# Sigmoid attention and a two-layer block with silu: h of batches 2 to 7 by pairs of batches in seven block products, with the next pair's attention in the out layer's time

## The chip, the core and the metric

The kernel runs on one core of one Trainium2 chip. The metric is the device time in microseconds; the kernel before takes 381.18 us (median of three runs, 381.03 to 382.37). Engines: TensorE (PE; PEld is its loading of weights), VectorE (DVE), ScalarE (ACT), GpSimd (POOL) and SyncE (SP). In this kernel GpSimd only issues loads, and SyncE issues stores and DMA transposes.

## What is computed

```python
# q, k, v: (8, 12, 448, 64) float32; w_in (768, 2048), w_out (2048, 768)
scores = q @ k.T / 8 - log(448)
attn   = sigmoid(scores)                  # no softmax
x      = (attn @ v), heads side by side   # (8 * 448, 768)
h      = x @ w_in
out    = (h * sigmoid(h)) @ w_out         # (3584, 768) float32
```

## The kernel before

**Attention.** The 12 heads of a batch are six pairs; a "quad" g is two pairs (three quads per batch, NQB = 24), and each quad has seven chunks of keys (NCH = 7), so a batch has 21 units (g, ch), NT_B. `scores` (L169) makes one unit: four matmuls of 64 x 64 x 448 into a tile of `ps_sc` (two PSUM buffers), and one Sigmoid on ScalarE (L183) into `attnT` (12 buffers). `values` (L193) takes the seven units of a quad, 28 matmuls into two tiles `pav` of `ps_1`, and VectorE copies them to `xT` (L218), scaled by 64. `ps_1` has four PSUM buffers for everything else. q and k of a quad must be transposed: for quads 0 to 5 by TensorE (L147); from 6 on by `dma_transpose` (L158): one copy into rows (`kr`, `qr`, three buffers) by ScalarE or VectorE, then a DMA transpose issued by SyncE into `kT`, `qT` (four buffers).

**h.** `h_unit` (L229) makes 128 columns of h for one batch: six matmuls (448 columns) into `ps_1`, a Sigmoid on ScalarE (L247), and the product on VectorE (L248) into `gTr`, which holds two batches.

**out.** `out_set` (L288) makes two 128-row blocks of out with seven block products of eight matmuls (384 columns) in place of eight, by sums of blocks: of g (`S1` to `S4`, VectorE, L318 to L327), of w_out (`T`, once, L277), and of the products (`plus`, L314, VectorE; one copy M1 by ScalarE, L321). Two batches have seven blocks, three sets; a seventh block is put into `kept` (L374) and forms a set with the next pair's.

**The order** is written out by hand, and each engine takes its instructions in that order. `all_moe` (L379) is a generator of h units and out sets; each `yield` gives the nanoseconds of one matmul (189 or 163). The main loop (L541) issues two units of scores, the values of a quad that is complete, a row copy if one is due, and then lets the generator run for `paces` nanoseconds (`stretch`, L398). So the attention of batch b + 1 is spread over the h and out of earlier batches. Before batch 2's scores (n = 42) stands one long stretch of 21500 ns, in which h of batches 0 and 1 ends; there ScalarE also copies the rows of quads 6, 7 and 8 (`by_h1`, L355), and VectorE makes the sums of w_out.

**Loads** go through GpSimd's queue in program order: after quad 2's values come v of quad 5, two quarters of w_out, then k and q of quads 6 and 7 (L449 to L454).

Of the kernel before, what the change touches and what calls it, by code (L numbers as in the profile page):

```python
# [2 lines left out]

# [14 lines left out]
def kernel(  # L18
# [9 lines left out]
    nc = tc.nc  # L28
# [93 lines left out]

    def new_qkT(g):
        for name in ("k", "q"):
            qkT[name, g] = p4.tile([P, NCH, P], F16, tag=f"{name}T", name=f"{name}T")

    dummy = cpool.tile([P, 512], F16, tag="dummy", name="dummy")

# [29 lines left out]
    def dma_transpose(g, name, copy):  # L158
        if ("k", g) not in qkT:
            new_qkT(g)  # L160
        rows = p3.tile([P, NCH, 2, D], F16, tag=f"{name}r", name=f"{name}r")
        copy(rows, flat[name, g].rearrange("p j c d -> p c j d"))  # L162
        nc.sync.dma_start_transpose(
            out=qkT[name, g], in_=rows.rearrange("p c j d -> p (c j d)")
        )
# [27 lines left out]
    def values(g, end=NCH):  # L193
        b, iq = divmod(g, NQ)
        if b not in xT:
            assert b < 2 or b - 2 in h_done
            xT[b] = p2.tile([P, NPAIR, S], F16, tag="xT", name="xT")
        pav, done_rounds = part_of.pop(g, None) or (
            [ps_1.tile([P, 512], F32, tag="ps1", name="pav") for _ in range(2)],
            0,  # L200
        )
        for ch in range(done_rounds, end):
            at = attnT.pop((g, ch))
            for half in range(2):
                own = slice(half * HP, (half + 1) * HP)
                for j in range(2):
                    nc.tensor.matmul(  # L207
                        pav[half][j * D : (j + 1) * D, :S],
                        flat["v", g][own, j, ch, :],
                        at[own, j, :],  # L210
                        start=(ch == 0),
                        stop=(ch == NCH - 1),
                    )
        if end < NCH:
            part_of[g] = pav, end
            return
        for half in range(2):
            nc.vector.tensor_scalar_mul(xT[b][:, half * NQ + iq, :], pav[half][:, :S], SX)  # L218
        if iq == NQ - 1:
            ready.add(b)  # L220

# [7 lines left out]
    def h_unit(b, fc):  # L229
        nonlocal hold  # L230
        hold = b > 0 and fc == NFC - 1
        ph = ps_1.tile([P, 512], F32, tag="ps1", name="ph")
        for at, cc in enumerate(pairs):
            assert b in ready or at < 4
            nc.tensor.matmul(  # L235
                ph[:, :S],
                w_in_sb[:, cc, fc * P : (fc + 1) * P],
                xT[b][:, cc, :],
                start=(at == 0),
                stop=(at == NCC - 1),  # L240
            )
            if at < NCC - 1:
                yield 189
        if fc == NFC - 1:
            h_done.add(b)
        tsig = p3.tile([P, S], F16, tag="tsig", name="tsig")
        nc.scalar.activation(tsig, ph[:, :S], AF.Sigmoid, bias=0.0, scale=ISX)  # L247
        nc.vector.tensor_mul(  # L248
            gTr[:, fc, (b % 2) * S : (b % 2) * S + S], ph[:, :S], tsig
        )  # L250
        yield 189

    rows_of = out.rearrange("(b p c) e -> b c p e", b=B, c=NCH)

# [27 lines left out]
    def block(g):  # L282
        return gTr[:, :, g * P : (g + 1) * P]
# [1 line left out]
    def row_blocks(m, g):  # L285
        return [rows_of[2 * m + u // NCH, u % NCH] for u in (2 * g, 2 * g + 1)]

    def out_set(a1, rows1, a2, rows2, last=False):  # L288
        nonlocal hold
        lo, hi = slice(0, NHC), slice(NHC, NFC)  # L290
        osb = [p4.tile([P, DMODEL], F32, tag="osb", name="osb") for _ in range(2)]
        c11, c12 = (osb[0][:, nh * NO2 : (nh + 1) * NO2] for nh in range(2))
        c21, c22 = (osb[1][:, nh * NO2 : (nh + 1) * NO2] for nh in range(2))
        m1 = p2.tile([P, NO2], F32, tag="m1", name="m1")
        sg = [cpool.tile([P, NHC, P], F16, tag=f"S{i}", name=f"S{i}") for i in range(1, 5)]

        def store(rows, o, cols, engines):
            for at, (row, eng) in enumerate(zip(rows, engines)):
# [1 line left out]

        left, right, whole = slice(0, NO2), slice(NO2, DMODEL), slice(0, DMODEL)

        def product(a, w):
            po = ps_1.tile([P, 512], F32, tag="ps1", name="po")
            for fc in range(NHC):
                nc.tensor.matmul(  # L306
                    po[:, :NO2], a[:, fc, :], w[:, fc, :], start=(fc == 0), stop=(fc == NHC - 1)
                )
                if fc < NHC - 1:
                    yield 163  # L310
            return po[:, :NO2]

        def plus(o, po, x, sign=ISX):
            nc.vector.scalar_tensor_tensor(  # L314
                out=o, in0=po, scalar=sign, in1=x, op0=ALU.mult, op1=ALU.add
            )

        nc.vector.tensor_sub(sg[2], a1[:, lo], a2[:, lo])  # L318
        nc.vector.tensor_add(sg[0], a2[:, lo], a2[:, hi])
        po = yield from product(a1[:, lo], wq[0][0])  # L320
        nc.scalar.activation(m1, po, AF.Copy, scale=ISX)  # L321
        nc.vector.tensor_sub(sg[1], sg[0], a1[:, lo])
        hold = False
        yield 163
        po = yield from product(a1[:, hi], wq[1][0])
        plus(c11, po, m1)
        nc.vector.tensor_sub(sg[3], a1[:, hi], sg[1])  # L327
        if last:
            store(rows1, osb[0], left, (nc.sync, nc.sync))
        yield 163  # L330
        po = yield from product(sg[2], tw[3])
        plus(c22, po, m1)
        yield 163
        po = yield from product(sg[1], tw[2])
        plus(c22, po, c22)
        plus(c12, po, m1)
        yield 163
        po = yield from product(a2[:, hi], tw[4])
        plus(c21, po, c22, -ISX)
        yield 163  # L340
        po = yield from product(sg[0], tw[1])
        plus(c22, po, c22)
# [9 lines left out]
        yield 163  # L352


    by_h1 = {3: 6, 6: 7, 9: 8}  # L355
    early = [h_unit(0, fc) for fc in range(2)]
    sums = w_sums()

    def moe_h(b):
        for fc in range(NFC):  # L360
            yield from early[fc] if b == 0 and fc < 2 else h_unit(b, fc)
            if b == 1:
                if fc >= 2:
                    next(sums)
                if fc in by_h1:
                    for name in ("k", "q"):
                        dma_transpose(by_h1[fc], name, act_copy)

    def moe_set(m, g):
        step = out_set(block(g), row_blocks(m, g), block(g + 1), row_blocks(m, g + 1))  # L370
        for i, ns in enumerate(step):
            if m % 2 == 0 and g == 2 and i % 8 == 4 and i < 32:
                fcs = slice(i // 8 * 4, i // 8 * 4 + 4)
                nc.scalar.activation(kept[:, fcs], block(NCH - 1)[:, fcs], AF.Copy)  # L374
            if m == 0 and g == 0 and i in (10, 14):
                next(sums)
            yield ns

    def all_moe():  # L379
        for m in range(B // 2):  # L380
            yield from moe_h(2 * m)
            if m > 0:
                yield from moe_set(m, 0)
            yield from moe_h(2 * m + 1)
            if m == 0:
                yield from moe_set(m, 0)
            yield from moe_set(m, 2)
            yield from moe_set(m, 4)
            if m % 2 == 1:
                g = NCH - 1  # L390
                yield from out_set(
                    kept, row_blocks(m - 1, g), block(g), row_blocks(m, g), m == B // 2 - 1
                )

    stream = all_moe()
# [44 lines left out]
    def after_values(g):  # L440
# [18 lines left out]
                load("kq", to)  # L459
        if g == 5:  # L460
            load("kq", 9)
        if g >= 6 and g + 3 < NQB:
            later.extend(((g + 3, "k"), (g + 3, "q")))

    later = []

    def rows_if_any():
        if later:
            g, name = later.pop(0)
            dma_transpose(g, name, nc.vector.tensor_copy)  # L470
            if name == "q" and g + 4 < NQB and g + 4 > 12:
                load("kq", g + 4)

    def values_if_any():
        if waiting:
            g = waiting.pop(0)
            values(g)
            after_values(g)

    keep_busy(9)  # L480
    pe_transpose(
# [23 lines left out]
    def begin(fc, steps):  # L505
        for _ in range(steps):
            next(early[fc])
# [28 lines left out]
        for do, *what in behind.get(n, ()):  # L536
            do(*what)

    paces = {1: 1600, 2: 2000, 3: 2550, 4: 3400, 5: 3400, 6: 3000, 7: 3000}
    stretch(paces[1])  # L540
    for n in range(NT_B + 3, len(units), 2):  # L541
        burst = units[n : n + 2]
        if n == 2 * NT_B:
            values_if_any()
            stretch(21500)
        for u in burst:
            scores(*u)
        values_if_any()
        rows_if_any()
        for g, ch in burst:  # L550
            if ch == NCH - 1:
                waiting.append(g)
        if n in (24, 30):
            transposes(4 + (n - 24) // 6, "k")
        elif n in (26, 32):
            transposes(4 + (n - 26) // 6, "q")
        stretch(paces[1] if 1 not in ready else paces[n // NT_B])
    for g in waiting:
        values(g)
    for _ in stream:  # L560
        pass

# [29 lines left out]
```

## Time and profile before

| | us |
|---|---|
| median of 3 runs | 381.18 |
| the profiled execution's time | 381.95 |
| its span | 380.2 |
| TensorE busy | 370.8 |
| VectorE busy | 235.2 |
| ScalarE busy | 225.9 |
| L235 (h), 768 matmuls, busy | 153.2 |
| L183 (Sigmoid of scores), 168 | 144.2 |
| L248 (product with the sigmoid), 128 | 78.9 |
| L247 (Sigmoid of h), 128 | 68.6 |
| L314 (sums of out's products), 112 | 60.7 |

The profile is one execution. Its span runs from the first to the last instruction, and the time has 1.75 us around it. Busy times count each instruction from start to end; matmuls overlap, so that 353 ns of a matmul of h are more than the distance from one to the next. The page cuts the span into 40 slices and gives the busy share of each in tenths. The chain of waits goes back from the last instruction, at each step to what released it. In a timeline, columns are start, duration, engine, line, operation, tiles and count; the brackets give the idle time before it and what ended it.

### The profile page before, as it was taken

What the parts mean: (1) busy time and instruction counts of PE and PEld (TensorE: products, weight loads), DVE (VectorE), ACT (ScalarE), POOL (GpSimd) and SP (SyncE); (2) the same over time, 40 slices, a digit from 0 to 9 for tenths busy, and PEclk for the clock granted to TensorE, in tenths of its full rate; (3) what the DMA queues carried; (4) which work ended last, traced back from release to release, by engine and by line L of the source; (5) the groups of instructions that cost most, each with busy time, mean ns of one, the idle gap of its engine ahead of it and who ended that gap; (6) DMA issues with size and microseconds to landing.
All of it is one profiled execution on the core that took longest, in us unless ns stands there. A gap on an engine that the chain in (4) does not pass through costs nothing.

```text
span 380.2 us, 7666 instructions
## 1 busy us (share of the span) xinstructions
PE 370.8 (98%) x3083; PEld 186.0 (49%) x3083; DVE 235.2 (62%) x416; ACT 225.9 (59%) x329; POOL 93.5 (25%) x158
## 2 busy tenths in 40 slices
PE   7989999999999999999999999999999999999995
PEld 2444445545554445445555444544455444555563
DVE  2636646987565666566766647735757446656773
ACT  4988875757667764777434576477764776054000
POOL 8946325403752323122221303101100000000000
PEclk9999999999999999999999999999999999999999
DMA  7999999995999947945939949536347300110233
GB/s 125 177 185 204 205 204 171 133 140 110 165 241 216 151 56 99 173 54 69 162 67 183 132 78 121 71 86 74 48 85 97 84 3 2 50 34 0 82 85 83
DMA packets 66403, 42.80 MB, mean 113 GB/s; under 512 B 37056, under 2 KB 62912, under 8 KB 66368
## 3 DMA queue, kind: packets, MB, share of 16 engines
q0 software_dynamic: 28032, 22.59, 43.2%
q1 hardware_dynamic: 38112, 19.41, 28.5%
q8 instruction: 24, 0.39, 0.4%
q10 hardware_dynamic: 224, 0.33, 0.3%
q14 instruction: 11, 0.09, 0.1%
HBM read 45.61 MB, written 11.01 MB: 149 GB/s over the span
## 4 chain that ended last, share of the span: by engine, by line
PE 78%; DMA 13%; POOL 3%; DVE 3%; ACT 2%; issue 1%; ACTq 0%; POOLq 0%
PE po L306 34%; PE ph L235 29%; PE psc L176 8%; PE pav L207 6%; DMA w_in_sb<-in_moe_w_in_dram 5%; DMA w_out_sb<-in_moe_w_out_dram 5%; DMA qf<-in_q_dram 1%; DMA vf<-in_v_dram 1%; POOL kf L78 1%; DVE gTr L248 1%; DVE T L277 1%; POOL qf L78 1%; ACT qr L137 1%; POOL vf L78 1%; ACT attnT L183 0%
## 5 line engine op out<-in xcount | busy, mean ns | idle before, releaser
L183 ACT ACTIVATE attnT<-psc 128x896 f16<-128x896 f32 x168 | 144.2, 918 | 59.9 <-PE psc L176 59.8
L235 PE MATMUL ph<-xT,w_in_sb 128*128 128x448 f16 x768 | 153.2, 353 | 1.2 <-DMA w_in_sb<-in_moe_w_in_dram 1.2
L248 DVE TENSOR_TENSOR gTr<-ph,tsig 128x448 f16<-128x448 f32 x128 | 78.9, 623 | 70.1 <-ACT tsig L247 68.6
L235 PEld LDWEIGHTS <-w_in_sb 128*128 128x128 f16 x768 | 71.9, 98 | 77.1 <-issue 12.8
L247 ACT ACTIVATE tsig<-ph 128x448 f16<-128x448 f32 x128 | 68.6, 547 | 54.4 <-PE ph L235 53.7
L78 POOL DMA_DIRECT2D vf<-in_v_dram x48 | 28.9, 624 | 136.4 <-PE pav L207 136.4
L306 PEld LDWEIGHTS <-S 128*128 128x128 f16 x448 | 42.3, 98 | 33.9 <-issue 6.8
L314 DVE SCALAR_TENSOR_TENSOR osb<-po,osb 128x384 f32<-128x384 f32 x70 | 37.6, 554 | 25.2 <-PE po L306 24.5
L176 PE MATMUL psc<-qT,kT 64*64 64x448 f16 x672 | 50.7, 362 | 0.9 <-ACT attnT L183 0.3
L218 DVE TENSOR_SCALAR xT<-pav 128x448 f16<-128x448 f32 x48 | 27.7, 619 | 31.4 <-PE pav L207 31.4
L306 PE MATMUL po<-T,S 128*128 128x384 f16 x224 | 40.6, 327 | 0.1
L306 PEld LDWEIGHTS <-gTr 128*128 128x128 f16 x304 | 28.7, 98 | 23.4 <-issue 5.0
L306 PE MATMUL po<-w_out_sb,S 128*128 128x384 f16 x224 | 39.9, 326 | 0.0
L207 PE MATMUL pav<-attnT,vf 64*64 64x448 f16 x672 | 37.5, 349 | 0.2 <-DVE gTr L248 0.2
L78 POOL DMA_DIRECT2D qf<-in_q_dram x46 | 27.7, 613 | 39.4 <-DVE qr L162 16.7
L306 PE MATMUL po<-w_out_sb,gTr 128*128 128x384 f16 x192 | 34.7, 327 | 0.0
L78 POOL DMA_DIRECT2D kf<-in_k_dram x50 | 30.3, 618 | 7.8 <-DVE kr L162 4.3
L176 PEld LDWEIGHTS <-kT 64*64 64x64 f16 x672 | 14.2, 104 | 31.0 <-issue 29.0
L207 PEld LDWEIGHTS <-vf 64*64 64x64 f16 x672 | 20.1, 107 | 12.3 <-issue 1.5
L314 DVE SCALAR_TENSOR_TENSOR osb<-po,m 128x384 f32<-128x384 f32 x42 | 23.1, 551 | 3.9 <-PE po L306 2.5
L306 PE MATMUL po<-T,gTr 128*128 128x384 f16 x112 | 21.4, 326 | 0.0
L321 ACT ACTIVATE m<-po 128x384 f32<-128x384 f32 x14 | 6.9, 492 | 24.0 <-PE po L306 24.0
(41 smaller groups left out, 130.8 us busy)
## 6 DMA issues: line engine op xcount, KB each, us to landing
out_dram<-osb SPq DMA_DIRECT2D x54, 192.0 KB, 3.0
vf<-in_v_dram POOLq DMA_DIRECT2D x48, 112.0 KB, 4.4
kf<-in_k_dram POOLq DMA_DIRECT2D x46, 112.0 KB, 5.4
qf<-in_q_dram POOLq DMA_DIRECT2D x46, 112.0 KB, 5.8
w_in_sb<-in_moe_w_in_dram POOLq DMA_DIRECT2D x4, 768.0 KB, 10.6
w_out_sb<-in_moe_w_out_dram POOLq DMA_DIRECT2D x4, 768.0 KB, 17.1
kT<-kr SPq DMA_TRANSPOSE x18, 5.8
qT<-qr SPq DMA_TRANSPOSE x18, 5.6
```

The lines of the kernel that those rows point to most:

```text
L78: nc.gpsimd.dma_start(flat[name, g][half * HP : (half + 1) * HP, :, c0:c1].rearrange("p i c d -> p i (c d)"), source[name][b, h0 : h0 + 2] ...
L137: nc.scalar.activation(o, i, AF.Copy)
L176: nc.tensor.matmul(psc[own, j, :S], qkT["k", g][rows, ch, own], qkT["q", g][rows, :, own], start=True, stop=True,)
L183: nc.scalar.activation(attnT[g, ch], psc[:, :, :S], AF.Sigmoid, bias=NEG_LOG_S, scale=QKSCALE)
L207: nc.tensor.matmul(pav[half][j * D : (j + 1) * D, :S], flat["v", g][own, j, ch, :], at[own, j, :], start=(ch == 0), stop=(ch == NCH - 1),)
L218: nc.vector.tensor_scalar_mul(xT[b][:, half * NQ + iq, :], pav[half][:, :S], SX)
L235: nc.tensor.matmul(ph[:, :S], w_in_sb[:, cc, fc * P : (fc + 1) * P], xT[b][:, cc, :], start=(at == 0), stop=(at == NCC - 1),)
L247: nc.scalar.activation(tsig, ph[:, :S], AF.Sigmoid, bias=0.0, scale=ISX)
L248: nc.vector.tensor_mul(gTr[:, fc, (b % 2) * S : (b % 2) * S + S], ph[:, :S], tsig)
L306: nc.tensor.matmul(po[:, :NO2], a[:, fc, :], w[:, fc, :], start=(fc == 0), stop=(fc == NHC - 1))
L314: nc.vector.scalar_tensor_tensor(out=o, in0=po, scalar=sign, in1=x, op0=ALU.mult, op1=ALU.add)
L321: nc.scalar.activation(m1, po, AF.Copy, scale=ISX)
```

## The change

For m = 1, 2, 3 the two batches of a pair form a 2 x 2 block problem: rows and columns of w_in in halves, x of the two batches as the other side. `h_pair` makes the eight blocks of h with seven products of three matmuls per 128 columns, with sums of w_in (`w_in_sums`, once, 12 operations of VectorE) and of x (`x_sums`, four subtractions per chunk pair, made when the second batch's values are done). The products go into PSUM on top of each other or are added by VectorE (`u2`, `u3`, `p1`); of each finished sum ScalarE makes one Silu. The last index's products stand within the first out product (`between`). The first out set of a pair takes its products in another order and finds its block sums made. Batches 0 and 1 keep the old h.

The attention of a pair's successor no longer runs beside h: the loop plans it into the out layer (`h_at`, `ends`, four units ahead), values come in two parts (four and three chunks), and ScalarE changes between the Sigmoid and the Silu function sets before and after each `h_pair`. The long stretch before batch 2's scores is 12500 ns, and rows of quads 6, 7 and 8 are copied after steps 0, 4 and 8 of h(1). Buffers: `kT`/`qT` 4 to 3, `kr`/`qr` 3 to 2, `osb` 4 to 3. `kept` is made by VectorE.

```diff
-            qkT[name, g] = p4.tile([P, NCH, P], F16, tag=f"{name}T", name=f"{name}T")
+            qkT[name, g] = p3.tile([P, NCH, P], F16, tag=f"{name}T", name=f"{name}T")
...
-        rows = p3.tile([P, NCH, 2, D], F16, tag=f"{name}r", name=f"{name}r")
+        rows = p2.tile([P, NCH, 2, D], F16, tag=f"{name}r", name=f"{name}r")
...
+    def x_sums(m, iq):
...
+        for o, x, y in ((t1, b12, b11), (t2, b22, t1), (t4, b21, t2), (t3, b22, b12)):
+            nc.vector.tensor_sub(o, x, y)
...
+    def w_in_sums():
...
+        for c in range(HCC):
+            nc.vector.tensor_add(sw[1][:, c], a21[:, c], a22[:, c])
+            yield
+            nc.vector.tensor_sub(sw[2][:, c], sw[1][:, c], a11[:, c])
+            yield
+            nc.vector.tensor_sub(sw[4][:, c], a12[:, c], sw[2][:, c])
+            yield
+        for c in range(HCC):
+            nc.vector.tensor_sub(sw[3][:, c], a11[:, c], a21[:, c])
+            yield
+
+    def h_pair(m, tail):
...
+        def late(i, y, z, p1, u2, u3):
+            silu(1, 1, i, u3)
+            if m < B // 2 - 1 and i < 4:
+                rows_of_quad(2 * NQ * (m + 1) + 1 + i // 2, "kq"[i % 2], act_copy)
+            yield from product(3, z, i, False)
+            nc.vector.tensor_add(u2, z, u2)
+            silu(0, 1, i, u2)
+            yield from product(4, y, i, False)
+            nc.vector.tensor_add(p1, y, p1)
+            silu(1, 0, i, p1)
...
+        def begin(i):
+            xb = ps_1.tile([P, 512], F32, tag="ps1", name="hx")[:, :S]
+            yield from product(1, xb, i, True)
+            p1 = p3.tile([P, S], F32, tag="m1", name="p1")
+            nc.scalar.activation(p1, xb, AF.Copy)
+            begun[i] = xb, p1
...
+        yield from begin(0)
+        for i in range(NHC):
+            end = i == NHC - 1
+            if not end:
+                yield from begin(i + 1)
+            xb, p1 = begun[i]
+            y = ps_sc.tile([P, 2, 512], F32, tag="pssc", name="hy")[:, 0, :S]
+            yield from product(6, y, i, True)
+            u2 = p3.tile([P, DMODEL], F32, tag="osb", name="u2")[:, :S]
+            nc.vector.tensor_add(u2, y, p1)
...
+            z = ps_1.tile([P, 512], F32, tag="ps1", name="hz")[:, :S]
+            yield from product(5, z, i, True)
+            if behind is not None and not end:
+                yield from late(*behind)
+            yield from product(2, xb, i, False)
+            silu(0, 0, i, xb)
+            yield from product(7, y, i, False)
+            u3 = cpool.tile([P, S], F32, tag="S2" if end else "S4", name="u3")
+            nc.vector.tensor_add(u3, y, p1)
...
+                nc.vector.tensor_add(u3, z, u3)
+            if end:
+                yield from late(*behind)
...
+            behind = i, y, z, p1, u2, u3
...
+        def rest():
+            yield from late(*behind)
+            nc.scalar.activation(warm, warm, AF.Sigmoid)
+            set_sums(0, EARLY, NHC)
+            set_sums(1, 0, NHC)
+            h_done.update((2 * m, 2 * m + 1))
...
-        osb = [p4.tile([P, DMODEL], F32, tag="osb", name="osb") for _ in range(2)]
+        osb = [p3.tile([P, DMODEL], F32, tag="osb", name="osb") for _ in range(2)]
...
-    by_h1 = {3: 6, 6: 7, 9: 8}
+    by_h1 = {0: 6, 4: 7, 8: 8}
...
+            if b == 0 and fc >= 7:
+                next(in_sums)
             if b == 1:
-                if fc >= 2:
+                if fc >= 4:
                     next(sums)
...
-                nc.scalar.activation(kept[:, fcs], block(NCH - 1)[:, fcs], AF.Copy)
+                nc.vector.tensor_scalar_mul(kept[:, fcs], block(NCH - 1)[:, fcs], scale)
...
-    paces = {1: 1600, 2: 2000, 3: 2550, 4: 3400, 5: 3400, 6: 3000, 7: 3000}
-    stretch(paces[1])
+    PACE, BURST, ROUND, SPARE = 1600, 590, 200, 2400
+    sets = 7 * NHC * 163
+    h_at = [(2 * NFC * NCC - 8) * 189 + 3 * sets]
+    for m in (1, 2):
+        h_at.append(h_at[-1] + 7 * NHC * HCC * 189 + (3 + m % 2) * sets)
+    AHEAD = 4
+    ends = [2 * NT_B, 4 * NT_B + AHEAD, 6 * NT_B + AHEAD, 8 * NT_B]
+    values_left = 2 * NT_B
+    stretch(PACE)
...
         if n == 2 * NT_B:
             values_if_any()
-            stretch(21500)
+            stretch(12500)
...
+                waiting.extend(((g, 0, NCH),) if n < 2 * NT_B else ((g, 0, 4), (g, 4, NCH)))
...
+        if n + 2 == ends[m]:
+            nc.scalar.activation(warm, warm, AF.Silu)
+        dense = h_at[m - 1] - SPARE - done
+        due = done
+        stretch((dense + values_left * ROUND) / ((ends[m] - n) // 2) - had * ROUND)
+        values_left -= had
+        if n + 2 == ends[m]:
+            while waiting:
+                values_if_any()
+                stretch(SPARE / 3)
+            values_left = 2 * NT_B
+            while 2 * m not in h_done:
+                done += next(stream)
+            due = done
+            stretch(3000)
```

## Prediction

> **What bounds the kernel now.** I read first the page's busy times and slices, then the chain that ended last in order of time, then TensorE's timeline.
>
> ```profile
> span 380.2 us, 7666 instructions
> PE 370.8 (98%) x3083; PEld 186.0 (49%) x3083; DVE 235.2 (62%) x416; ACT 225.9 (59%) x329; POOL 93.5 (25%) x158
> PE   7989999999999999999999999999999999999995
> PEclk9999999999999999999999999999999999999999
> ```
>
> TensorE (PE) is full from the second slice to the last at an undiminished granted clock; VectorE (DVE) and ScalarE (ACT) stand near 60%. The end of the chain of waits gives the price of a matmul where nothing else runs:
>
> ```profile
> 330.33 18.16 PE ph L235 x96
> 348.49 27.31 PE po L306 x168
> ```
>
> 18.16/96 = 189.2 ns for one of 448 columns (h), 27.31/168 = 162.6 ns for one of 384 (out). These are the planner's 189 and 163. The 353 and 327 ns that the page gives as means overlap. So a matmul taken away is worth its 189 ns if nothing else stops TensorE.
>
> **What is removed.** A pair of batches has 2 x 16 x 6 = 192 h matmuls; seven products over 8 index steps and 3 row blocks make 7 x 8 x 3 = 168. Three pairs save 72: 72 x 189.2 ns = **-13.6 us**, all on TensorE's path.
>
> **VectorE and ScalarE in the product phase.** One index step is 21 matmuls, 3.97 us. VectorE gets five sums per step. None is in the trace; nearest are L248 (448 columns from PSUM, 623 ns) and L314 (384 float32 columns from PSUM and SBUF):
>
> ```profile
> L248 DVE TENSOR_TENSOR gTr<-ph,tsig 128x448 f16<-128x448 f32 x128 | 78.9, 623 | 70.1 <-ACT tsig L247 68.6
> L314 DVE SCALAR_TENSOR_TENSOR osb<-po,osb 128x384 f32<-128x384 f32 x70 | 37.6, 554 | 25.2 <-PE po L306 24.5
> ```
>
> 554 + 64 columns at (684-548)/256 = 0.53 to 1.04 ns gives 590 to 620; I take 620, so 3.1 us of 3.97. ScalarE gets one copy and four Silu (nearest: L247, 547 ns): 2.8 us, 3.7 with one of L137's row copies (0.94), which the first four steps of pairs 1 and 2 have. Bounds for a Silu: 0.44 (L247 when it follows another) to 0.92 (L183, twice the columns). At 0.55 both engines lie beside TensorE. The tightest order is: product 7 of step i, then two sums, then product 3 of step i in the next step. Products 1, 6 and 5 lie between, 1.70 us; the sums need 0.16 (a 353 ns matmul overhangs its 189) + 0.62 + 0.54 (VectorE back to back) + some 0.15 for two semaphores = 1.47. It fits, by 0.2 us. At the edges (last values before the sums of x; last silu before the out layer's block sums) I count 0.6 to 1.7 us of such chains against 1.1 to 1.75 us of matmuls; **+0.5** for three pairs, bounds 0 to 4.
>
> At each edge ScalarE also changes its function set, six loads more; the trace's only load (L422) took 1283 ns. After h the first out sum waits for the Sigmoid load and the copy of M1, but four PSUM buffers cover this: the copy ends some 0.75 us before the fifth product wants M1's buffer. The Trainium skill (ScalarE: Activation LUTs, "What ACT_TABLE_LOAD costs") gives about 1380 ns of drain on top of each 1283. By that the copy would end 0.65 us too late, and the sum would have 3 x 0.65 = 2.0 us more; no second load is in this trace to check it.
>
> **The early part, h of batch 1.** The scores of batch 2 were issued after 21.5 us of h, now after 12.5. They need quad 6 transposed, and its data is late. From the timelines of GpSimd (loads), ScalarE (row copies), SyncE (transposes) and TensorE, in this order:
>
> ```profile
> 44.29 1.21 POOL L78 DMA_DIRECT2D kf<-in_k_dram  x2
> 48.42 0.60 POOL L78 DMA_DIRECT2D qf<-in_q_dram  x1 [2.92 <-DMA w_out_sb<-in_moe_w_out_dram]
> 52.29 0.59 POOL L78 DMA_DIRECT2D qf<-in_q_dram  x1 [3.27 <-DMA w_out_sb<-in_moe_w_out_dram]
> ...
> 63.15 0.94 ACT L137 ACTIVATE kr<-kf 128x896 f16<-128x896 f16 x1
> 63.99 0.94 ACT L137 ACTIVATE qr<-qf 128x896 f16<-128x896 f16 x1
> ...
> 64.11 1.30 SPq L163 DMA_TRANSPOSE kT<-kr  x1
> 65.51 1.99 SPq L163 DMA_TRANSPOSE qT<-qr  x1
> ...
> 57.39 18.90 PE L235 MATMUL ph<-xT,w_in_sb 128*128 128x448 f16 x99
> 79.22 0.57 PE L176 MATMUL psc<-qT,kT 64*64 64x448 f16 x8
> ```
>
> The tile view gives 17.2 us to landing for both k halves (62.1), and 14.2 and 10.9 for the q halves (62.6, 63.2). GpSimd's queue is unchanged up to there. The change asks ScalarE for these rows behind step 0 of h(1), about 59.8, three steps earlier than before. ScalarE takes its work in order, so it waits until 62.1, then until 63.2, and is through at 64.1; the sigmoids of steps 1 to 4 queue behind it. Step 5 reuses step 1's PSUM: wanted at 63.6, free after sigmoid and product at 65.3. **+1.7** (0 if the loads land earlier).
>
> 12.5 us of h from 57.39 then end at 57.39 + 12.5 + 1.7 = 71.6, and the scores ask for qT 6. The rows are ready at 63.0 and 64.2; before, kT took 7.7 us to land and qT 12.5 (78.0, just ahead of the scores at 79.22). The hardware queue moved 2278 packets from 66 to 78, 190 per us; two transposes are 2 x 7 x 128 = 1792. From 65.0 that is 9.4 us: 74.4. **+2.8** of standing still; bounds 0 (if each needs the 3.1 us that one took at 81.8, when the loads had ended) and 6.4 (landing at 78.0 as before).
>
> Quad 8's rows, now with two buffers instead of three, wait for quad 6's transpose to land; ScalarE holds its sigmoids meanwhile and is 1.75 us behind when scores start. **+1.0**, bounds 0 to 1.75. Twelve W sums of 683 ns fall mostly into h(0), where VectorE works 10.7 us of 20: **+0.3** (0 to 1).
>
> **The out layer with the next pair's attention.** I count by units of scores, TensorE against VectorE. TensorE: matmuls as above, a unit of scores 0.25 us (half of 79.22 to 79.72), a round of values 0.19. VectorE: eight L314 and four block sums per set (7.16 us), xT copies 0.62, x sums 0.38 (line through 768 at 548 and 1024 at 684 ns), row copies 0.61, parts of kept 0.5, remaining sums of W and T.
>
> Pair 0 (units 42 to 87): TensorE 53.1, VectorE 49.8, ScalarE 46 x 0.918 + 4.5 = 46.7.
> Pair 1: 54.9 against 44.9 and 40.6. Pair 2: 44.8 against 38.6 and 36.4.
>
> VectorE's timeline shows three L314 from 102.31 and the next operation at 103.90, 0.53 us each instead of 0.554, and other pairs start 0.46 to 0.60 us apart, so its true load is some 10% lower. From 101.78 to 107 of the old out stage it ran without a gap and TensorE did not stop. The longest new lump, two xT copies and four x sums, is 2.3 us; the four PSUM buffers cover two products, 2.6 us. **+1.0** for three windows, bounds 0 to 6. The values come in two parts now, so their two PSUM buffers are held for some 4.1 us (two bursts and the copies) and out has the other two meanwhile; each of its products is 1.3 us of matmuls, and a sum follows within that unless it meets the lump. osb with three buffers instead of four waits for a store of some 3.0 us (section 6 of the page) against 3.9 us of products: nothing. kept (8 x 0.63 us) leaves ScalarE, which then has only scores and one copy per set. Rows of quads 13, 14, 19 and 20 and their transposes move into the h phases, where SyncE's queue holds the last set's stores at most and the data were loaded a stage before; their four to seven microseconds of landing lie under 31.8 us of h: nothing.
>
> Removed with the old order: one wait of 0.3 us for attnT at 143.67, **-0.3**.
>
> **Sum.** -13.6 + 1.7 + 2.8 + 1.0 + 0.3 + 0.5 + 1.0 - 0.3 = -6.6 us. The profiled execution took 381.95 us (span 380.2), so 375.3; the median of the runs, 381.18, is 0.77 lower: **374.6**.
>
> **Rivals.**
> *All is hidden.* The transposes of quad 6 run faster once asked for earlier and only edges remain: -13.6 + 1 to 3 us, 368.6 to 370.6. For it: 82 to 84 us shows 1000 packets per us. Against: that is after the loads end. 0.20.
> *The product phase runs at VectorE's or ScalarE's pace.* If every sum waits alone (0.62 + 0.2), a step is 4.1 us; with a Silu at 0.92 it is 4.2. 24 steps x 0.14 to 0.25 = 3.3 to 6 us: 378 to 380.6. For it: 0.2 us of margin in the order. Against: L248 and L247 alternate in h now with half a microsecond idle each. 0.16.
> *VectorE becomes the bound of the out layer* (slower). Its 133.3 us stand in 152.8 us of TensorE's. It decides if VectorE must idle for results: from 76 to 115 it was busy 28.3 of 39, idle 27%. With that share kept, the windows take 133.3/0.73 = 183 us, 30 more: 405. The run is slower by over 0.5% (1.9 us) from 133.3/(1-x) > 152.8 + 8.5, x above 17%; at 20% it is 388. Against: the idle time was spent waiting for TensorE, and vanishes when VectorE is behind (101.78 to 107). 0.08.
>
> **Chances.** Forecast (371 to 378): 0.56; the rivals as given. Faster by over 0.5% (below 379.3; about what a measurement of this kernel can tell from no change): 0.56 + 0.20 + 0.01 = 0.77; within: 0.15; slower: 0.08. The range, 368.5 to 380.5, leaves out the slow rival and the ends of the others.
>
> **What would show it.** In the profile after: 3011 matmuls and the h phases of 31.8 us without gaps (right) or with a stop ahead of each product 3 (second rival); a gap of TensorE near 64 with ScalarE waiting for a load; a wait of the first scores of batch 2 for DMA, ending near 74; VectorE without gaps in out windows while TensorE waits (third rival). A h phase longer than 33 us, or scores of batch 2 that wait past 78, would make the forecast wrong.

## The result, and the profile after

The changed kernel takes 384.91 us (median), the kernel before 381.35 us on the same chip: a ratio of 1.0062 [1.0039, 1.0085], slower by 0.6%. The forecast was 374.6 us with 0.77 on faster; time and sign were wrong. Ratios, here and below, leave out the runs more than 1.5% above the fastest of their kernel (here four, the profiled one of 388.05 us and one of 458.1 us at a granted clock of 0.754, whose cause is not known, among them); medians do not. The first experiment below has a profile of an execution of 383.96 us, and the account of the time is made on that one.

From the page of the changed kernel (line numbers are its own: L177 makes scores, L243 h of batches 0 and 1, L309 the block products of h, L457 out):

```profile
span 386.3 us, 7672 instructions
PE 364.6 (94%) x3011; PEld 181.6 (47%) x3011; DVE 261.0 (68%) x491; ACT 254.2 (66%) x368; POOL 93.1 (24%) x158
PE   7989998599995799999999999999999999999995
PEclk9999999879999699999999999999999999999999
L177 PE MATMUL psc<-qT,kT 64*64 64x448 f16 x672 | 52.1, 370 | 11.6 <-DMA qT<-qr 11.1
```

72 matmuls are gone (3083 to 3011). But two holes are new in TensorE's row, slice 8 and slices 13 and 14 (a slice is 9.66 us: 68 to 77, and 116 to 135), and in and behind them the granted clock falls. The group of scores gives the name: 11.6 us idle, 11.1 of them until a `qT` came by DMA. In the page before no slice was below 9 from the fourth to the last but one. TensorE's timeline at the holes:

```profile
65.38 6.40 PE L243 MATMUL ph<-xT,w_in_sb 128*128 128x448 f16 x33 [1.82 <-DVE gTr L256]
76.48 0.96 PE L177 MATMUL psc<-qT,kT 64*64 64x448 f16 x8 [4.69 <-DMA qT<-qr]
77.37 3.92 PE L243 MATMUL ph<-xT,w_in_sb 128*128 128x448 f16 x10
...
120.86 0.38 PE L177 MATMUL psc<-qT,kT 64*64 64x448 f16 x4
127.63 0.59 PE L177 MATMUL psc<-qT,kT 64*64 64x448 f16 x4 [6.38 <-DMA qT<-qr]
128.15 3.38 PE L457 MATMUL po<-w_out_sb,gTr 128*128 128x384 f16 x10
```

Three stops: 1.82 us at 65, 4.69 before 76.48 (quad 6, the first scores of batch 2), 6.38 before 127.63 (quad 11). After the second, ten matmuls of h take 3.92 us where ten take 1.9 at 189 ns; after the third, ten of out take 3.38 where ten take 1.6. The windows show why (width, TensorE's busy time and count, then weights, VectorE, ScalarE, GpSimd, the granted clock, mean DMA share and GB/s):

```profile
75.00:80.00 5.00, 3.52 (x16) 1.26 (x16) 1.09 (x2) 3.43 (x5) 0.59 (x1) 0.50 1.36 153
125.00:130.00 5.00, 2.37 (x10) 1.06 (x11) 0.32 (x1) 0.92 (x1) 2.36 (x4) 0.60 1.34 172
```

In stretches from 76.4 to 81.7 and from 127.6 to 132.9 the clock is 0.51: 5.3 us each at half pace, 2.6 us lost each time *after* the wait is over.

The chain of waits (start, duration, what) shows the two transposes with their times from issue to landing, and the block products:

```profile
64.51 11.93 DMA qT<-qr
112.88 14.62 DMA qT<-qr
153.59 1.14 PE hz L309 x6
157.56 1.14 PE hz L309 x6
161.54 1.14 PE hz L309 x6
```

One index step of the products is 3.97 us, as predicted: the new arithmetic runs at TensorE's pace. ScalarE's timeline has the 1.82 us at 65 and one of the changes of function set:

```profile
62.15 0.95 ACT L138 ACTIVATE kr<-kf 128x896 f16<-128x896 f16 x1 [2.54 <-DMA kf<-in_k_dram]
63.29 0.95 ACT L138 ACTIVATE qr<-qf 128x896 f16<-128x896 f16 x1 [0.19 <-DMA qf<-in_q_dram]
64.15 1.82 ACT L255 ACTIVATE tsig<-ph 128x448 f16<-128x448 f32 x4
...
178.74 0.58 ACT L320 ACTIVATE gTr<-p 128x448 f16<-128x448 f32 x1
179.34 1.28 ACT L394 ACT_TABLE_LOAD   x1
180.63 0.20 ACT L394 ACTIVATE warm<-warm 128x1 f32<-128x1 f32 x1
```

The copy of quad 6's k rows stood 2.54 us for its load, and four sigmoids of h, ready before, ran only after it.

### The profile page after: what moved, and what is told of

It is laid out like the page before. It is cut to its first block, busy times and chain, and to the rows that moved or that the text cites. A ratio compares the mean times of both kernels' runs of the same rounds, so it can differ in the third digit from the quotient of the medians.

```text
span 386.3 us, 7672 instructions
## 1 busy us (share of the span) xinstructions
PE 364.6 (94%) x3011; PEld 181.6 (47%) x3011; DVE 261.0 (68%) x491; ACT 254.2 (66%) x368; POOL 93.1 (24%) x158
## 4 chain that ended last, share of the span: by engine, by line
PE 69%; DMA 22%; POOL 4%; issue 2%; DVE 2%; ACT 0%; SPq 0%; DVEq 0%; ACTq 0%; POOLq 0%
PE po L457 30%; PE hy L309 11%; PE psc L177 7%; PE hx L309 7%; PE hz L309 7%; DMA qT<-qr 7%; PE pav L208 5%; DMA qf<-in_q_dram 5%; DMA w_out_sb<-in_moe_w_out_dram 4%; DMA w_in_sb<-in_moe_w_in_dram 3%; PE ph L243 2%; POOL kf L79 2%; DMA vf<-in_v_dram 1%; DMA out_dram<-osb 1%; POOL vf L79 1%
## 5 line engine op out<-in xcount | busy, mean ns | idle before, releaser
L177 PE MATMUL psc<-qT,kT 64*64 64x448 f16 x672 | 52.1, 370 | 11.6 <-DMA qT<-qr 11.1
L79 POOL DMA_DIRECT2D vf<-in_v_dram x48 | 28.8, 616 | 127.0 <-PE pav L208 75.6
L457 PEld LDWEIGHTS <-S 128*128 128x128 f16 x448 | 40.9, 98 | 37.1 <-issue 12.1
L243 PE MATMUL ph<-xT,w_in_sb 128*128 128x448 f16 x192 | 41.2, 365 | 2.5 <-DVE gTr L256 1.8
L208 PE MATMUL pav<-attnT,vf 64*64 64x448 f16 x672 | 42.0, 352 | 0.8 <-DVE osb L467 0.5
L457 PE MATMUL po<-T,S 128*128 128x384 f16 x224 | 41.8, 327 | 0.0
L457 PE MATMUL po<-w_out_sb,S 128*128 128x384 f16 x224 | 41.5, 327 | 0.0
L457 PEld LDWEIGHTS <-gTr 128*128 128x128 f16 x304 | 28.4, 99 | 26.2 <-issue 9.6
L309 PEld LDWEIGHTS <-w_in_sb 128*128 128x128 f16 x288 | 28.1, 98 | 26.5 <-issue 0.4
L320 ACT ACTIVATE gTr<-u 128x448 f16<-128x448 f32 x48 | 27.6, 575 | 19.4 <-DVE u L329 14.8
L457 PE MATMUL po<-w_out_sb,gTr 128*128 128x384 f16 x192 | 37.8, 337 | 0.0
L177 PEld LDWEIGHTS <-kT 64*64 64x64 f16 x672 | 16.0, 105 | 41.9 <-issue 38.9
L309 PE MATMUL hy<-xs,w_in_sb 128*128 128x448 f16 x144 | 35.1, 353 | 0.1
L309 PE MATMUL hx<-xT,w_in_sb 128*128 128x448 f16 x144 | 34.6, 353 | 0.0
L256 DVE TENSOR_TENSOR gTr<-ph,tsig 128x448 f16<-128x448 f32 x32 | 19.4, 621 | 21.6 <-ACT tsig L255 21.4
L467 DVE SCALAR_TENSOR_TENSOR osb<-po,m 128x384 f32<-128x384 f32 x42 | 22.9, 551 | 14.1 <-PE po L457 10.0
L309 PEld LDWEIGHTS <-W 128*128 128x128 f16 x216 | 21.1, 98 | 19.6
## 6 DMA issues: line engine op xcount, KB each, us to landing
w_in_sb<-in_moe_w_in_dram POOLq DMA_DIRECT2D x4, 768.0 KB, 10.6
```

The costliest lines, as they stand in the source:

```text
L79: nc.gpsimd.dma_start(flat[name, g][half * HP : (half + 1) * HP, :, c0:c1].rearrange("p i c d -> p i (c d)"), source[name][b, h0 : h0 + 2] ...
L177: nc.tensor.matmul(psc[own, j, :S], qkT["k", g][rows, ch, own], qkT["q", g][rows, :, own], start=True, stop=True,)
L208: nc.tensor.matmul(pav[half][j * D : (j + 1) * D, :S], flat["v", g][own, j, ch, :], at[own, j, :], start=(ch == 0), stop=(ch == NCH - 1),)
L243: nc.tensor.matmul(ph[:, :S], w_in_sb[:, cc, fc * P : (fc + 1) * P], xT[b][:, cc, :], start=(at == 0), stop=(at == NCC - 1),)
L256: nc.vector.tensor_mul(gTr[:, fc, (b % 2) * S : (b % 2) * S + S], ph[:, :S], tsig)
L309: nc.tensor.matmul(ps, a[:, c, i * P : (i + 1) * P], bs(c), start=(first and c == 0), stop=(c == HCC - 1), skip_group_check=True,)
```

## The experiments

Each time stands beside runs of the kernel before on the same chip; all edits are to the changed kernel, except in e7 and e8. The theory: TensorE waits for two transposes that come too late, and pays a second time by a slow clock. The rivals: the time is lost in the out layer or at the edges of the products; or DMA traffic, not standing still, slows the clock.

### The same kernel again (e9_unchanged, run with e10 and e11, told first)

> The changed kernel as it is, on the chip of this group, for comparison: 383 to 386, clock 0.98 to 0.99, waits of 2 us or more for the transposes of quads 6 and 11.

384.11 us (382.6 to 388.08); ratio 1.0079 [1.0046, 1.0112]. Its profiled execution took 383.96 us (span 382.2). TensorE's timeline has the same stops:

```profile
74.25 0.96 PE L177 MATMUL psc<-qT,kT 64*64 64x448 f16 x8 [2.79 <-DMA qT<-qr]
123.76 0.59 PE L177 MATMUL psc<-qT,kT 64*64 64x448 f16 x4 [6.36 <-DMA qT<-qr]
```

With the stop behind ScalarE at 65 (1.55) and the slow clock behind both waits (0.50 from 74.2 to 77.3 and from 123.8 to 128.3: 1.5 and 2.3 us lost), the difference of its span from the one before, 382.2 - 380.2 = +2.0, is -13.6 + 1.55 + 2.79 + 1.5 + 6.36 + 2.3 = +0.9, and a remainder of 1.1 us, which holds the edges of the products, the out layer and the chance differences of two executions (the first 57 us ran 0.34 us faster here). So most of the account is closed: a gain of the predicted size, and 14.5 us of stops and slow clock at two places. In the stretch behind the second wait VectorE does nothing and ScalarE half, so that neither can be what slows TensorE there:

```profile
125.00:130.00 5.00, 5.00 (x38) 2.13 (x36) 0.00 (x0) 2.57 (x4) 1.18 (x2) 0.65 1.37 168
```

### Dummies in the waits (e1_fill)

```diff
             stretch(12500)
+            keep_busy(20)
...
+            if u == (11, 0):
+                keep_busy(28)
             scores(*u)
```

The dummies are matmuls on a constant tile, work that the output doesn't use.

> The changed kernel with matmuls on constant data put ahead of its two longest waits of TensorE: 20 of 512 columns ahead of the first scores of batch 2, 28 ahead of the first scores of quad 11; nothing is added to the output. Theory (two waits for DMA transposes, 4.7 and 6.4 us, and behind each a stretch at half the granted clock): the waits stay but are filled, the clock stays at 1.00, and only the slow matmuls behind them are saved. 10 matmuls of h took 3.85 us in place of 1.89 and 10 of out 3.31 in place of 1.63, with scores beside them some 2.5 and 2.2 us: 384.9 - 4.7 = 380.2, with a smaller spread from run to run. Rival (the clock falls for another reason than TensorE's standing still): 384 to 386, clock below 0.99 as before.

384.17 us (383.51 to 385.75); 1.0085 [1.0056, 1.0114]. The expected 380.2 was missed; the time lies in the rival's range, but the clock doesn't. TensorE's timeline:

```profile
119.13 6.22 PE L135 MATMUL pw<-dummy 128*128 128x512 f16 x28
125.59 1.80 PE L457 MATMUL po<-w_out_sb,gTr 128*128 128x384 f16 x10
```

The second half of the theory holds: with the wait filled, the ten out matmuls behind it take 1.80 us and not 3.38, and the granted clock of the execution is 1.00 (0.994 to 1.00 in the four runs). But 4.48 + 6.22 = 10.7 us of dummies are as long as the longest waits, and they are spent in every run: what the clock gives, they take. The runs lie closer together (2.2 us of spread in four runs against 5.5 in e9's eight). Filling a wait is no cure.

### A longer stretch, deferred loads, and both (e2_late, e3_defer, e4_both)

e2 gives quad 6 more time:

```diff
-            stretch(12500)
+            stretch(17500)
```

> The changed kernel with the long stretch of h ahead of batch 2's scores at 17500 ns in place of 12500. Theory: the scores ask for quad 6 at 76.8 us, when it has landed (76.5), so the first wait and its slow clock go, 4.7 + 2.5 us; the wait for quad 11 stays or grows, since the bursts lie closer: 377 to 380. Rival (VectorE or ScalarE bound the out layer of pair 0, whose share of TensorE work per burst shrinks): the time lost comes back there, 383 to 386.

385.26 us (381.79 to 386.95); 1.0094 [1.0063, 1.0124]: missed. The time lies in the rival's range. The wait for quad 6 is gone, but TensorE stops 1.80 us at 65, as in the changed kernel, behind ScalarE's wait for quad 6's load, and 1.48 us at 76 behind ScalarE, which holds the copy of quad 8's rows until a row buffer is free, that is until quad 6's transpose has landed; then 3.16 us at 101 and 4.35 for quad 11. The first three end with VectorE, which waits for ScalarE in the first two, as the rival has it; but both engines stood there for data. The one at 101, in TensorE's timeline:

```profile
101.13 0.48 PE L457 MATMUL po<-w_out_sb,gTr 128*128 128x384 f16 x1 [3.16 <-DVE osb L467]
```

VectorE stood there in a row copy of quad 10 whose load had not landed (6.17 us), with the sums of out queued behind it. In the changed kernel VectorE waits there too (3.70 us at 102), unseen by TensorE; with the long stretch 5 us longer it shows.

e3 takes traffic away from quad 11's transpose. The loads of quads 13 to 15 are asked for after the first scores of quad 11, not behind the row copies of quads 9 to 11:

```diff
-            load("kq", g + 4)
+            if g < 12:
+                put_off.append(g + 4)
+            else:
+                load("kq", g + 4)
...
+            if u == (11, 0):
+                for g in put_off:
+                    load("kq", g)
```

> The changed kernel with the loads of q and k of quads 13, 14 and 15 issued after the first scores of quad 11 instead of right behind the row copies of quads 9, 10 and 11. Theory (the transpose of quad 11 lands 14.6 us after its issue because loads that are not yet needed fill the DMA engines): it lands in 4 to 8 us, the second wait and its slow clock go, 6.4 + 2.2 us: 376 to 377. Rival (the transpose is slow for its own sake, or the wait merely moves to the next quad): 383 to 386.

378.28 us (375.22, 376.53, 380.03 and 386.63); 0.9897 [0.9837, 0.9958]; the profiled execution took 375.22, at a clock of 1.00. Expected was 376 to 377, 1.3 us below the median. Quad 11's `qT` now lands 5.2 us after its issue at 109.12, not 14.6 after 112.88, and its scores don't wait. One edit in the order of loads turns the sign. What is left in TensorE's timeline:

```profile
74.67 0.57 PE L177 MATMUL psc<-qT,kT 64*64 64x448 f16 x8 [2.96 <-DMA qT<-qr]
```

Here the clock stayed at 1.00 behind a wait of 2.96 us.

e4 is e2 and e3 together.

> The changed kernel with both edits: 17500 ns and the later loads of quads 13 to 15. Theory (two waits account for nearly all of the missing gain): 369 to 371, clock 0.995 or more. Rival (VectorE or ScalarE hold the out layer up once the waits are gone): above 376, with gaps of TensorE that end with VectorE or ScalarE between 85 and 145 us.

378.68 us (376.28 to 382.45); 0.9914 [0.9893, 0.9936]; the expected 369 to 371 was missed. The longer stretch keeps its own stops; the profiled execution, of 382.45 us, is the longest of the ten, and the largest stop in its TensorE timeline is:

```profile
77.41 3.74 PE L243 MATMUL ph<-xT,w_in_sb 128*128 128x448 f16 x12 [3.24 <-DVE gTr L256]
```

That chain is VectorE behind ScalarE behind quad 8's buffer: the step that the prediction priced at +1.0. TensorE also stops 2.89 us at 104 behind VectorE, as in e2. A later deadline for quad 6 only hands its late transpose on to the next user of the buffer.

### Quad 6 earlier (e5_early6)

```diff
-    by_h1 = {0: 6, 4: 7, 8: 8}
+    by_h1 = {4: 7, 8: 8}
...
+            if b == 0 and fc == 13:
+                for name in ("k", "q"):
+                    dma_transpose(6, name, act_copy)
...
+            load("kq", 6)
             load_w_out(1, 0)
...
-            load("kq", 6)
```

> The changed kernel with q and k of quad 6 loaded ahead of the last two quarters of w_out instead of behind them, and its rows copied after step 13 of h of batch 0 instead of step 0 of batch 1; the stretch stays at 12500. Theory (the root of the first wait is that quad 6 is loaded late and behind w_out): ScalarE's wait for the load with TensorE's 1.8 us at 64, and the 4.7 us at 72 with its slow clock go; the second wait, for quad 11, stays: 376 to 379, clock 0.99. Rival (its transposes are slow for the load of the DMA engines whenever they are issued there): 382 to 385.

381.58 us (379.09 to 384.42); 0.9997 [0.9967, 1.0026]. The waits at 65 and 76 are gone, small ones of 2.0 us in all come between 57 and 61, and quad 11's stays (6.60 us). Against e9's 384.11 (on another chip) that is 2.5 us less; the account of e9 asks for 1.55 + 2.79 + 1.5 - 2.0 = 3.8. Expected were 376 to 379: missed by 3 us.

### Both causes removed (e6_all, e10_no_ahead)

e6 is e3 and e5 together, and quads 10 to 12 are loaded earlier, for VectorE's wait in e2:

```diff
-        if g == 6:
-            for to in (10, 11, 12):
-                load("kq", to)
...
+        if n in (44, 48, 52):
+            load("kq", 10 + (n - 44) // 4)
```

> The changed kernel with early loads and rows of quad 6 as above, the loads of quads 13 to 15 behind the first scores of quad 11, and those of quads 10, 11 and 12 at the bursts of units 44, 48 and 52 instead of behind quad 6's values, so that no row copy of VectorE waits for them. Theory (what the change lacked was data in time, nothing else): no wait of TensorE over 1 us after 30 us, clock 1.00 in nearly every run: 367 to 370, and runs within 1 us of each other. Rival (VectorE or ScalarE bound the out layer of pair 0): 373 or more, with waits of TensorE that end with VectorE or ScalarE and no load behind them.

372.55 us (371.51 to 377.36); 0.9761 [0.9723, 0.98], faster than both kernels. From its page (span 369.7):

```profile
PE 359.0 (97%) x3011; PEld 180.2 (49%) x3011; DVE 261.2 (71%) x491; ACT 254.0 (69%) x368; POOL 93.3 (25%) x158
PE   7989998999999999999999999999999999999995
PEclk9999999999999999999999999999999999999999
```

The holes and the dents in the clock are gone; the longest stop of TensorE after 30 us is 0.60 us. Quad 11's transposes land in 4.4 and 3.7 us. Quad 6's take no less (10.6 and 14.1, among the loads), but are asked for at 55 to 56 and are there at 70.55. The span is 3.1 us above 380.2 - 13.6 = 366.6, so edges and out layer cost at most that; 2.1 us of it are stops of 0.6 us and less between 57 and 71. That answers the first rival. The expected 367 to 370 was too low by 2.5 us, and the runs lie 5.9 us apart, not within 1.

e10 is e6 without the last diff.

> The version with all three edits of the loads, but q and k of quads 10 to 12 again loaded behind quad 6's values. Theory (VectorE waits in its order for quad 10's rows some 3.8 us, and TensorE feels it only where its PSUM buffers run out): 1 to 4 us more than with the early loads, 373 to 376.5, a wait of TensorE for VectorE's sums near 98. Rival (that wait of VectorE is covered in full): 372 to 373.

372.15 us (371.29 to 374.16); 0.9755 [0.9726, 0.9785], the same. The rival of that run was right: with the stretch of 12500, VectorE's wait for quad 10 is covered. The edits of e3 and e5 are all that is needed; against the unchanged kernel on the same chip they take 12.0 us off.

### How much delay costs (e11_rows15)

```diff
-            if b == 0 and fc == 13:
+            if b == 0 and fc == 15:
```

This is e6 with the rows of quad 6 two steps later, 3.5 us.

> The version with all three edits of the loads, quad 6's rows copied after step 15 of h of batch 0 instead of step 13. Theory: ScalarE's 1.9 us of row copies no longer stand ahead of the last scores of batch 1, so TensorE's waits of 1.0 us for them near 57 go; quad 6's transpose lands some 2 us later, near 70, when its scores ask for it: 370.5 to 372.5. Rival (it lands after they ask): a wait of 1 to 4 us with a slow clock, 373 to 378.

377.3 us (375.62 to 383.29); 0.9869 [0.9844, 0.9894]: 5.2 us more than e10 (the same chip; e6 and e10 differ by 0.4) for 3.5 us of delay. TensorE's timeline:

```profile
74.35 0.96 PE L177 MATMUL psc<-qT,kT 64*64 64x448 f16 x8 [5.23 <-DMA qT<-qr]
```

The wait is back and the clock behind it is 0.50 from 75 to 80. The theory that the delay would only eat slack (370.5 to 372.5) fell, the rival (373 to 378) held.

### What standing still costs by itself (e7_gap9, e8_gap16)

These are the *kernel before*, with 9 or 16 extra copies of a constant tile on ScalarE behind the scores at n = 140, where the DMA engines have nearly nothing to do. The copies are extra work; the output doesn't use them.

```diff
+            if n == 140:
+                for _ in range(9):
+                    nc.scalar.activation(dummy, dummy, AF.Copy)
```

> The kernel before, with nine extra copies of a constant tile by ScalarE (some 4.8 us of its time, not part of the output) behind the scores of unit 141: TensorE stands still once, for 1 to 2.5 us, until ScalarE frees PSUM. Theory (the granted clock is halved after some 3 us of standing still): the clock stays at 1.00, and the time rises by the gap alone, 382 to 383.5.

385.66 us (385.22 to 386.2); 1.0105 [1.0069, 1.0141], more than the expected 382 to 383.5. In the profiled execution TensorE stood 2.47 and then 0.20 us. Ahead of the gap it was 0.73 us earlier than in the trace before, at the last stage of h 3.57 us later (333.90 against 330.33): 4.3 us lost, 1.6 more than it stood, which is what half a clock takes in the 3.3 us from 276.4 to 279.7. The timeline and a window behind the gap:

```profile
274.98 1.46 PE L306 MATMUL po<-w_out_sb,gTr 128*128 128x384 f16 x8 [2.47 <-DVE gTr L248]
```

```profile
277.00:280.00 3.00, 3.00 (x17) 1.00 (x16) 2.46 (x5) 2.81 (x5) 0.00 (x0) 0.55 0.13 27
```

What the clock alone costs isn't settled by this run. In two of the four runs the granted clock of the whole execution is 1.000, and they took no less (385.22 and 385.96). ScalarE, which is late by its extra copies, is busy 2.81 of the 3 us behind the gap and VectorE 2.46, so at full clock TensorE might have stood for them instead; no trace shows it.

> The same with 16 copies, 8.5 us of ScalarE: TensorE stands still for 5 to 6 us. Theory (halved after some 3 us, for several us): the granted clock shows 0.5 behind the gap, and the time rises by 2 us or more beyond the gap: 388 to 390, with a wider spread. Rival (the slow stretches of the changed kernel come from DMA traffic, which beside them is heavy): the clock stays at 1.00 and the time rises by the gap alone, 386 to 387.

390.87 us (390.06 to 391.69); 1.0241 [1.0203, 1.0279]; expected 388 to 390. The gap is 7.09 us and the loss, counted in the same way, 8.7 (0.56 and 8.12): again 1.6 more. Timeline and window:

```profile
279.77 2.72 PE L306 MATMUL po<-w_out_sb,gTr 128*128 128x384 f16 x8 [7.09 <-DVE gTr L248]
```

```profile
280.00:283.00 3.00, 3.00 (x11) 1.32 (x9) 2.96 (x6) 2.95 (x5) 0.00 (x0) 0.51 0.00 0
```

Eight matmuls that need 1.3 us take 2.72, while the DMA share is 0.00: the clock falls because TensorE stood, not because transfers run. So the rival on DMA traffic fell, and in both profiled executions one standing cost its length and 1.6 us, whether it lasted 2.5 or 7.

## Why the prediction was wrong

**Right.** The -13.6 us: 3011 matmuls, 3.97 us per index step. The engines beside them: Silu 529 ns from PSUM and 575 from SBUF (assumed 550), a sum of h 624 ns (assumed 620), so the second rival, a product phase at the pace of VectorE or ScalarE, did not come. The sum, from the groups by shape:

```profile
L379 DVE TENSOR_TENSOR u<-hy,p 128x448 f32<-128x448 f32 x24 | 15.0, 624 | 13.1 <-PE hy L309 13.0
```

The third rival, VectorE as the bound of the out layer, did not come either: where VectorE is full (4.96 of 5 us from 120 to 125), TensorE waits for `qT`, and in e6, without that wait, TensorE is at 97% with the same VectorE work. ScalarE behind quad 6's load: predicted 1.7, measured 1.55 and 1.82. The wait for quad 6: predicted +2.8, measured 2.79 in e9 and 4.69 in the other execution, and its end near 74 (74.25 in e9, 76.44 in the other; that e9 meets +2.8 to 0.01 us is chance). The function set's loads: 1283 ns each, and at 179.34 the load starts 0.02 us after the Silu ends, and the next activation starts 0.01 us after the load. The 2.0 us that the Trainium skill's drain (ScalarE: Activation LUTs, "What ACT_TABLE_LOAD costs") would have added don't show. Neither of the two signs that the prediction named for a wrong forecast came: the h phases take 32.6 to 32.9 us, and the scores of batch 2 wait until 76.5.

**The step that failed: "The out layer with the next pair's attention".** It set TensorE against VectorE and ScalarE (pair 0: 53.1, 49.8 and 46.7) and left out the DMA engines. Of rows and transposes it followed only those that move into the h phases and called them "nothing". Quad 11's stay in the out layer, and there the deadline moved: the scores of batch 2 begin 2.7 us earlier (76.48 for 79.22) and their bursts stand 2.6 us apart instead of 3.1 (17 of them up to 120.86 for 132.07), so quad 11's scores, the second half of a burst, ask at 121.2 and not at 132.3. The trace before, SyncE's and TensorE's timelines:

```profile
118.10 1.45 SPq L163 DMA_TRANSPOSE qT<-qr  x1
...
132.07 0.57 PE L176 MATMUL psc<-qT,kT 64*64 64x448 f16 x8
```

The transpose did not move along: it landed at 127.0 before (118.10 + 8.9) and at 127.5 after (112.88 + 14.6). It was issued 5.2 us sooner and took 5.7 longer, because the loads of quads 13 to 15 go behind the row copies of 9 to 11 and fill the same time (GpSimd issues them from 106 to 120); e3, which moves only them, brings it to 5.2 us. The landing at 127.0 stood in the trace before, and the new time of asking followed from the plan of units. What the runs showed in place of "nothing": a wait of 6.4 us.

**The second failure: the price of standing still.** Every stop was taken at its length. Behind both waits TensorE runs at half clock for 3 to 5 us, 1.5 to 2.6 us each; e7 and e8 give 1.6 in the kernel before with idle DMA engines, though not with idle ScalarE and VectorE. In the trace before no stop was long enough to show it. Price: 3.8 us in e9, 5.2 in the other execution.

**Terms below the forecast.** Quad 8's rows (+1.0) cost TensorE nothing visible in the changed kernel; the cause is real and shows in e2 and e4, when quad 6 is asked for later. W sums, edges and out layer, less the wait that went, were counted at 1.5; the remainder of e9 is 1.1, or 1.4 with the 0.34 us of the early part set apart, so this term was about right.

With the two failures the sum of the prediction, -6.6, comes to -6.6 + 6.4 + 3.8 = +3.6, less 1.0 + 0.4 for those terms and 0.15 for ScalarE's wait: +2.0, the difference of the spans in e9. It closes to the last tenth because the 1.1 is the remainder of that same difference. The slow rival named the right side and the wrong engine: what bounded the out layer for 6.4 us was a transfer.

**Open.** The kernel's runs spread over 7 us where the kernel before spreads over 2; of the 4.1 us between the two profiles 1.9 lie in the wait for quad 6, 1.4 in the clock behind the waits and 0.3 in ScalarE's wait. Why quad 6's transpose landed at 74.2 in one and at 76.4 in the other is not known.

## What to carry to other kernels

When a change makes a stage shorter, write down for each transfer that the stage uses when it lands and when it will now be asked for; a transfer that was early by 5 us is late when the stage moves up by 11, and loads that are triggered by the work that got faster crowd it further. Price a stop of TensorE of 2.5 us or more at its length and half of the slow stretch that may follow, 1.5 to 2.6 us in these traces (one stop of 2.96 us had none). If a transfer is late, ask for it earlier or move the traffic around it: a later deadline only moved the stop to the next user of its buffer, and filling the stop with dummies cost what it saved.

## What the runs showed of the hardware

- The granted clock falls to 0.50 behind a standstill of TensorE, and stays there for 3 to 5 us of work. In e7 it was still 1.00 for the first 1.4 us behind the gap of 2.47 us, then 0.50 from about 276.3 to 279.7; two other runs of e7 have 1.000 as a whole. A gap of 2.96 us in e3 left it at 1.00. The Trainium skill (TensorE: Matmul & The Clock Gate, "What's actually happening") has the half clock come after an idle window of about 3.4 us and last about as long, with a window that runs freely, so that results differ from run to run. The length agrees with e7 (3.4 us), less so with the 5.3 us of the changed kernel, and the differing with e3; the bound doesn't agree, since 2.47 us were enough in e7.
- A transpose of 128 x 896 from SBUF to SBUF landed in 3.7 to 6.1 us where the loads had been moved away (e3 and e6, quad 11) and in 11.7 to 14.6 us among loads (the changed kernel and e9, quad 11). While they were under way, the queue of the loads (software_dynamic) moved 0.33 MB in 6.9 us and 0.23 in 6.6 in the first two, 1.55 in 14.6 and 1.29 in 14.1 in the others. The total doesn't tell them apart: 290 GB/s in e3 from 105 to 110, 172 in the changed kernel from 125 to 130.
- A row copy that waits for its load blocks its engine, and everything queued behind it: 2.54 us on ScalarE in the changed kernel, with four sigmoids behind it, and up to 3.7 us on VectorE.
